# Attention's small products in halves, splits and reloads behind the last fold, and one pool of five PSUM banks

## The chip, the cores and the metric

The kernel runs on one core of one Trainium2 chip. The metric is device time in microseconds; lower is better. TensorE (PE) multiplies into PSUM, which has eight banks of 128 x 512 floats; VectorE (DVE) and ScalarE (ACT) read PSUM and write SBUF; GpSimd (POOL) works on SBUF alone; SyncE (SP) and the queues of ACT and POOL issue transfers.

## The reference

For 4 batches of 768 tokens and 8 heads of 64, each chunk of 32 tokens attends to 8 memory keys, 16 tokens to its left, itself and 8 to its right. The result, 512 channels wide, goes through a mixer along the tokens (rank 32) and a two-layer perceptron with 2048 hidden units:

```python
for c in range(nc):
    l_start, r_end = max(0, c_start - 16), min(S, c_end + 8)
    k_full = np.concatenate([mem_k, k[:, :, l_start:r_end]], axis=2)
    v_full = np.concatenate([mem_v, v[:, :, l_start:r_end]], axis=2)
    scores = scale * np.matmul(q_c, k_full.transpose(0, 1, 3, 2))
    a = softmax(scores)
    out[:, :, c_start:c_end] = np.matmul(a, v_full)
x = out.transpose(0, 2, 1, 3).reshape(B, S, H * D)
u = x + (x.transpose(0, 2, 1) @ U @ V).transpose(0, 2, 1)
return u + np.maximum(u @ w_ch1, 0.0) @ w_ch2
```

The weights arrive as 64-bit floats and are decoded on the chip.

## The kernel before

**Precision.** Each factor of the perceptron is split into a high and a low part (`split_hidden`, the pairs `th`/`tl`, `w1`/`w1l`), and three products are added in PSUM.

**Batches.** Batch 0's attention runs first and alone. Then `both_blocks` does batch 0's perceptron in 32 units, one for each token block (2) and hidden chunk (16): `w1_step` (12 matmuls, L1124), then `w2_step` of an earlier unit (nine matmuls: six L1178, three L1183). Batches 1 to 3 go through `fast(b)`: a scheme of seven products for the first projection. `products(p)` is a group of seven products of six matmuls each (L1412) for the hidden chunks 2p and 2p+1, into three banks; p runs from 0 to 7. `first_block(p)` adds their second projection for the first token block, `second_block` that for the other block, eight hidden chunks at a time, in three accumulators that live for the whole pass.

**The next batch's attention is a generator**, run a step at a time between these pieces, at *borders*. In `both_blocks` a border stands before and after `w1_step` of the units behind the 18th, and `PLAN` says how many steps each gets. In `fast` there are 40 borders: after the third and the seventh product of each group, and after each `w2_step`; `PLACES` lists those that get a step. For T = 0, 1, 2 (256 tokens each) the steps are: transposes of keys and queries (`k_part`, `q_part`, L583), scores and softmax (`s_part`), transposes of the weights (`weights_in`, L742), and weighted values (`weigh`, `av_part`). In `fast(1)` and `fast(2)`: `weigh(0)` at border 16, `s_part(1)` at 18, `q_part(2)` at 20, `weights_in(1)` at 22, `s_part(2)` at 23 (behind the last `w2_step` of `second_block`'s first pass), `weigh(1)` at 24 (behind the third product of p = 4), `weights_in(2)` at 25, `weigh(2)` at 27.

**Small products.** `s_turn` and `av_turn` each run 64 matmuls of 64 x 32 by 64 x 64 into two banks in turn (L657, L760); a trace holds two records for each, 128 in a set. There are 24 sets, 18 of them for batches 1 to 3. Behind the scores VectorE takes a maximum (L675) and a difference (L676) over each whole bank, ScalarE the exponential, VectorE the sums.

**The end of batch 0.** `prepare` makes the sums of weight chunks for the seven products, `build_factor` splits one of them (L1380 on ACT, L1381 on DVE). `recall(0, 1)` reloads the three tiles of x that the last second projection adds to (SP, L1114). `following()` drains the attention of batch 1 and then folds its tokens (`fold_both`, transposes L1333, parts L1343, `th` L1347, `tl` L1348), one third in each of the last three units; `fast(1)`'s products read `th` and `tl`.

**Order.** PE, POOL and SP run in the order of the program. DVE is ordered by hand until unit 18 and ACT until unit 2; from there a planner orders both by when inputs should be ready and by priority (`tc.high_priority`).

**PSUM.** Three banks (`ps_o`) hold accumulators. Two (`ps_h`) serve `w1_step`, two of the three banks of `products` and two of `second_block`'s accumulators; three (`ps_a`) serve attention's `att_ps`, the third bank of `products` and the other accumulators:

```python
ps_a = ctx.enter_context(tc.tile_pool(name="ps_a", bufs=3, space=PSUM))
ps_h = ctx.enter_context(tc.tile_pool(name="ps_h", bufs=2, space=PSUM))
ps_o = ctx.enter_context(tc.tile_pool(name="ps_o", bufs=1, space=PSUM))
```

Of the kernel before, what the change touches and what calls it, by code (L numbers as in the profile page):

```python
# [55 lines left out]
def chunk_attn_then_mixer_kernel(  # L56
# [46 lines left out]
    late = left.enter_context(tc.tile_pool(name="late", bufs=1))  # L103
    early = right.enter_context(tc.tile_pool(name="early", bufs=1, side="right"))
    dram = ctx.enter_context(tc.tile_pool(name="dram", bufs=1, space=bass.MemoryType.DRAM))
    ps_a = ctx.enter_context(tc.tile_pool(name="ps_a", bufs=3, space=PSUM))
    ps_h = ctx.enter_context(tc.tile_pool(name="ps_h", bufs=2, space=PSUM))
    ps_o = ctx.enter_context(tc.tile_pool(name="ps_o", bufs=1, space=PSUM))

    def slot(shape, dtype, name):  # L110
# [14 lines left out]
    def bank():  # L125
        kind = next(kinds, "a")
        if kind == "a":
            return ps_a.tile([P, 512], F32, name="ps_a")
        if kind == "h":
            return ps_h.tile([P, 512], F32, name="ps_h")  # L130
        return ps_o.tile([P, 512], F32, name="acc" + kind[1])

    warm, small = [0], [0]
# [292 lines left out]
    def attention(b, xs):  # L426
# [109 lines left out]
        def v_home(T):  # L536
            return vbs[T if b == 0 else T % 2]
# [107 lines left out]
        pT = {}  # L645

        def s_turn(T):

            qt = [qts.pop((T, h)) for h in range(2)]
            banks = [att_ps() for _ in range(2)]  # L650
            psv = [ps.rearrange("n (t k g w) -> n t k g w", t=2, k=2, g=2) for ps in banks]
            for t in range(2):
                for p in range(NPR):
                    for i in range(NI):
                        for s in range(2):
                            rows = slice(D * s, D * s + D)
                            nc.tensor.matmul(  # L657
                                out=psv[s][CK * i:CK * i + CK, t, p % 2, p // 2, :],
                                lhsT=qt[p // 2][rows, p % 2, NI * t + i, :],
                                rhs=kall[rows, NB * (T % 2) + NI * t + i, p, :], start=True, stop=True,  # L660
                            )
            return banks, psv

        def s_weights(T, banks, psv, which=range(2)):
            for s in which:
# [64 lines left out]
            nc.vector.reciprocal(out=rs, in_=rs)  # L730

        def s_part(T):
            s_weights(T, *s_turn(T))
            s_sums(T)
            s_recip(T)

        def t_part(T, s):
            pt = pts[T, s]
# [6 lines left out]
            nc.scalar.copy(out=pT[T, s], in_=psv)  # L745

        def av_part(T):
            x_part(T, av_turn(T))

        def av_turn(T):  # L750

            vt, pt = v_home(T), [pT.pop((T, s)) for s in range(2)]
            banks = [att_ps() for _ in range(2)]
            psv = [ps.rearrange("n (t j d) -> n t j d", t=2, j=4) for ps in banks]
            for t in range(2):
                for j in range(4):
                    for i in range(NI):
                        for g in range(2):
                            rows = slice(NW * g, NW * g + NW)
                            nc.tensor.matmul(  # L760
                                out=psv[g][CK * i:CK * i + CK, t, j],
                                lhsT=pt[j % 2][rows, 2 * t + j // 2, CK * i:CK * i + CK],
                                rhs=vt[rows, NI * t + i, D * j:D * j + D], start=True, stop=True,
                            )
            return psv

        def x_part(T, psv):
            rs = rss.pop(T)
# [171 lines left out]
        else:  # L940
# [13 lines left out]
            def weigh(T):  # L954
                need("v", T)
                av_part(T)
                issued.add(f"av{T}")

            def weights_in(T):
                for s in two:  # L960
# [22 lines left out]
                (weigh, (1,)), (weights_in, (2,)),  # L983
            )
            for what, args in order:
                what(*args)
                yield
            weigh(2)
            yield

        if b > 0:
            gp.append(att_ps())
# [53 lines left out]
    w1ls = {}  # L1046

    def turn_x(c):
        bank_ = ps_h.tile([P, 512], F32, name="ps_h") if c in (1, 2) else ps_o.tile([P, 512], F32, name=f"acc{int(c == 0)}")
        for tt in range(TB):  # L1050
            nc.tensor.matmul(
                out=bank_[:, tt * P:(tt + 1) * P], lhsT=xs[(0, tt)][:, c * P:(c + 1) * P],
                rhs=ident, start=(tt == 0), stop=False, is_transpose=True, skip_group_check=True,
            )
        return bank_
# [59 lines left out]

    def w1_step(b, blk, f, w1l):
        uh, ul = uT[(b, blk)]
        ph = att_ps() if f == 0 and (b, blk) == (0, 0) else ps_h.tile([P, 512], F32, name="ps_h")
# [30 lines left out]
    def w2_step(b, blk, f, where, begins, ends, hh, hl):  # L1149

        if begins:
            for tt in range(TB):
                if where == 1 or where == 2 and tt == 2:
                    accs[where, tt] = ps_a.tile([P, CH], F32, name="ps_a")
                elif where == 2:
                    accs[where, tt] = ps_h.tile([P, CH], F32, name="ps_h")
# [35 lines left out]
    def both_blocks(following):  # L1192
# [11 lines left out]
        for n, (blk, f, where, begins, ends) in enumerate(units):  # L1204
# [28 lines left out]
                open_turned()  # L1233
            if n == len(units) - 1:
                open_fast()
                for m in (3, 4):
                    build_factor(0, m)
            if n == 0:
                decode(2, 4)
                for c, g3 in rest[2:]:  # L1240
# [9 lines left out]
                border()  # L1250
            if n == len(units) - 3:
                prepare(0, True)
            if n == len(units) - 2:
                recall(0, 1)
            if n >= len(units) - 3:
                following()
            prev.append((blk, f, where, begins, ends) + hid_)
            if solo or n % 2 == 0 or ends:
                while len(prev) > (not ends):
# [5 lines left out]
    def place(n):  # L1265
        for _ in range(n):
            next(gen[0], None)
# [5 lines left out]

    at = [0]

    def border():
        place(PLAN[at[0]])
        at[0] += 1

# [86 lines left out]
    def fast_border():  # L1366
        let_go()
        serve(4)
        place(PLACES.count(passed[0]))
        passed[0] += 1  # L1370

# [21 lines left out]
    def seven(b, kept, last):  # L1393
# [3 lines left out]
        made = {}  # L1397

        def products(p):
            banks = [ps_h.tile([P, 512], F32, name="ps_h"), ps_a.tile([P, 512], F32, name="ps_a")]  # L1400
            banks.append(ps_h.tile([P, 512], F32, name="ps_h"))
# [148 lines left out]
```

## Time and profile before

| what | value |
|---|---|
| median of 3 runs | 652.95 us (651.62 to 653.56) |
| the profiled execution's own time | 654.24 us |
| its span, first to last instruction | 652.5 us |
| mean granted TensorE clock | 0.992 of 2.4 GHz |
| busy: PE, DVE, ACT, POOL | 625.3, 422.9, 305.5, 75.4 us |

The profile is of one execution. Busy time is a share of the span; a matmul's end is modelled, and matmuls overlap, so starts are compared rather than sums of durations. "L1412" is line 1412 of the kernel before. A wait is the idle time of an engine before an instruction, put down to what released it; "issue" means that nothing in the profile released it. Times in rows are microseconds from the span's start.

### The profile page before, as it was taken

To read this page: it belongs to the slowest core of one execution; us is meant where nothing else is said; L and a number is where in the kernel's file an instruction comes from. 1 tells how busy PE (TensorE), PEld (TensorE's weight loads), DVE (VectorE), ACT (ScalarE), POOL (GpSimd) and SP (SyncE) were. 2 spreads that over 40 slices of the span, in tenths; PEclk is the share of its full clock that TensorE was granted. 3 is DMA by queue.
4 is the path that set the end of the run, shared out by engine and by line. 5 is a ranking of instruction groups with operands and counts; after the bars stand their busy time and mean duration, and the time that the engine had idled before them with its cause. 6 is when DMAs were issued, how large, how long until landed. Compare 5 with 4: busy or idle time off the path is not lost.

```text
span 652.5 us, 15750 instructions
## 1 busy us (share of the span) xinstructions
PE 625.3 (96%) x6196; PEld 547.6 (84%) x6198; DVE 422.9 (65%) x889; ACT 305.5 (47%) x770; POOL 75.4 (12%) x128
## 2 busy tenths in 40 slices
PE   7788999999899899999999999999999999999997
PEld 6656999988778799878898899888988899889986
DVE  5977997887428957458676863655756875427442
ACT  4656676585215555524334554533433643315321
POOL 4700011100200722033300000000000000000000
PEclk9999999999989999999999999999999999999999
DMA  8896685695606589233361589144432663100011
GB/s 215 188 334 242 207 272 177 193 271 150 180 18 207 162 218 225 86 89 128 128 212 70 149 209 247 43 99 130 156 93 78 206 220 91 49 23 26 2 73 73
DMA packets 134357, 96.83 MB, mean 148 GB/s; under 512 B 88842, under 2 KB 111114, under 8 KB 134282
## 3 DMA queue, kind: packets, MB, share of 16 engines
q1 hardware_dynamic: 121690, 70.25, 38.9%
q10 hardware_dynamic: 9936, 17.04, 7.0%
q0 software_dynamic: 2656, 8.52, 3.9%
q8 instruction: 49, 0.80, 0.5%
q14 instruction: 26, 0.21, 0.1%
HBM read 69.44 MB, written 25.43 MB: 145 GB/s over the span
## 4 chain that ended last, share of the span: by engine, by line
PE 79%; DVE 7%; DMA 5%; issue 3%; ACT 3%; SPq 1%; POOL 0%; ACTq 0%; DVEq 0%; POOLq 0%
PE ps_h L1412 18%; PE acc L1178 13%; PE ps_a L1412 7%; PE ps_h L1124 6%; PE acc L1183 6%; PE ps_h L1178 6%; PE ps_a L1178 4%; PE ps_h L1183 3%; PE ps_a L760 2%; PE ps_a L583 2%; PE ps_a L657 2%; PE ps_a L1183 2%; PE ps_a L742 1%; DMA vb<-in_v_dram 1%; PE ps_h L1170 1%
## 5 line engine op out<-in xcount | busy, mean ns | idle before, releaser
L1178 PE MATMUL acc<-w,hh 128*128 128x512 f32 x366 | 98.5, 404 | 1.0 <-DVE w L368 1.0
L1412 PE MATMUL ps_h<-th,w1l 128*128 128x384 f32 x288 | 83.3, 342 | 2.6 <-DVE part L1429 2.6
L1178 PEld LDWEIGHTS acc<-w,hh 128*128 128x128 f32 x366 | 67.6, 190 | 15.7 <-issue 1.7
L1388 DVE SCALAR_TENSOR_TENSOR hl<-kept,hh 128x384 fp32r<-128x384 f32 x48 | 26.8, 558 | 48.9 <-PE ps_a L1183 22.4
L1412 PEld LDWEIGHTS ps_h<-th,w1l 128*128 128x128 f32 x288 | 52.8, 188 | 6.8 <-DVE part L1429 4.1
L1387 ACT ACTIVATE hh<-kept 128x384 fp32r<-128x384 f32 x48 | 25.4, 530 | 62.8 <-PE ps_a L1178 39.2
L1412 PE MATMUL ps_h<-th,s 128*128 128x384 f32 x192 | 53.0, 337 | 0.0
L1183 PE MATMUL acc<-w,hl 128*128 128x512 f32 x183 | 52.3, 394 | 0.0
L1412 PE MATMUL ps_h<-tl,w1l 128*128 128x384 f32 x144 | 48.6, 338 | 1.8 <-DVE tl L1348 1.8
L1178 PE MATMUL ps_h<-w,hh 128*128 128x512 f32 x156 | 43.0, 397 | 0.0
L1124 PE MATMUL ps_h<-uh,w1h 128*128 128x384 f32 x124 | 42.2, 346 | 0.5 <-ACT uh L1096 0.5
L1183 PEld LDWEIGHTS acc<-w,hl 128*128 128x128 f32 x183 | 34.8, 190 | 7.6
L1124 PE MATMUL ps_h<-ul,w1h 128*128 128x384 f32 x124 | 40.9, 337 | 0.0
L1178 PE MATMUL ps_a<-w,hh 128*128 128x512 f32 x132 | 37.9, 390 | 1.7 <-ACT hh L1130 1.7
L1418 ACT COPY part<-ps_h 128x384 f32<-128x384 f32 x24 | 11.5, 480 | 54.2 <-PE ps_h L1412 38.8
L1380 ACT CAST s<-sums 128x256 fp32r<-128x256 f32 x72 | 28.2, 409 | 16.6 <-PE ps_h L1412 16.6
L1412 PEld LDWEIGHTS ps_h<-th,s 128*128 128x128 f32 x192 | 35.1, 188 | 0.2 <-DVE part L1422 0.2
L1300 POOL TENSOR_TENSOR sums<-val 128x256 f32<-128x256 f32 x40 | 31.8, 818 | 28.3 <-PE ps_a L583 10.7
L1420 DVE TENSOR_TENSOR part<-ps_a,part 128x384 f32<-128x384 f32 x24 | 13.3, 554 | 31.3 <-PE ps_a L1412 29.5
L1178 PEld LDWEIGHTS ps_h<-w,hh 128*128 128x128 f32 x156 | 28.4, 188 | 5.6
L1381 DVE TENSOR_TENSOR s<-sums,s 128x256 fp32r<-128x256 f32 x72 | 32.6, 464 | 0.0
L1412 PE MATMUL ps_h<-tl,s 128*128 128x384 f32 x96 | 32.3, 336 | 0.0
(279 smaller groups left out, 1400.8 us busy)
## 6 DMA issues: line engine op xcount, KB each, us to landing
sums<-sumsd SPq DMA_DIRECT2D x32, 256.0 KB
xd<-x ACTq DMA_DIRECT2D x30, 256.0 KB
x<-xd SPq DMA_DIRECT2D x30, 256.0 KB
rw<-in_moe_w_ch_dram SPq DMA_DIRECT2D x14, 512.0 KB
vb<-in_v_dram SPq DMA_DIRECT2D x56, 98.0 KB
raw<-in_moe_w_ch_dram SPq DMA_DIRECT2D x20, 256.0 KB
qn<-in_q_dram SPq DMA_DIRECT2D x36, 128.0 KB
rw<-in_moe_w_ch_dram SPq DMA_DIRECT2D x16, 256.0 KB
```

Of the source, the lines that this page charges most:

```text
L583: nc.tensor.transpose(out=psv[:, p, r, :], in_=half[:, r, 2 * p:2 * p + 2, :].rearrange("n h d -> n (h d)"), identity=ident,)
L657: nc.tensor.matmul(out=psv[s][CK * i:CK * i + CK, t, p % 2, p // 2, :], lhsT=qt[p // 2][rows, p % 2, NI * t + i, :], rhs=kall[rows, NB * ( ...
L1124: nc.tensor.matmul(out=ph[:, :TOK], lhsT=w[:, c, :], rhs=u[c], start=(m == 0), stop=(m + 1 == len(parts)),)
L1178: nc.tensor.matmul(out=acc[tt], lhsT=h[:, sl], rhs=w, start=(begins and m == 0), stop=False,)
L1183: nc.tensor.matmul(out=acc[tt], lhsT=hl[:, sl], rhs=w2h[f], start=False, stop=ends is not None)
L1300: nc.gpsimd.tensor_tensor(out=two[:, m % 2], in0=a, in1=b_, op=getattr(ALU, op))
L1380: nc.scalar.copy(out=s[:, 0:2], in_=total)
L1381: nc.vector.tensor_tensor(out=s[:, 2:4], in0=total, in1=s[:, 0:2].bitcast(F32), op=ALU.subtract)
L1387: nc.scalar.activation(out=hh, in_=src, func=AF.Relu)
L1388: nc.vector.scalar_tensor_tensor(out=hl, in0=src, scalar=0.0, in1=hh.bitcast(F32), op0=ALU.max, op1=ALU.subtract,)
L1412: nc.tensor.matmul(out=banks[at_], lhsT=w[:, wc, :], rhs=t[:, i, c, :], start=(n < 3 and m == 0), stop=(m + 1 == len(parts)), skip_group_c ...
L1420: nc.vector.tensor_tensor(out=ta, in0=b2, in1=ta, op=ALU.subtract)
```

## The change

It does three things.

1. For batches 1 to 3, `s_part` and `av_part` run only the first half of their small products (`half(0)`, 32 matmuls); the second half and all that follows it (softmax, or the scaling of x) go on a list, `tails`, that is run at the next border, before that border's own step. Batch 0 runs both halves in one go, as before.
2. In the last unit of `both_blocks`, the reloads `recall(0, 1)` (one unit earlier before) and the splits `build_factor(0, 3)` and `(0, 4)` stand behind `following()`.
3. The pools `ps_a` and `ps_h` become one pool of five banks, `ps_b`. All places that took a tile of either take one of `ps_b` with the tag "bank" (`bank`, `turn_x`, `w1_step`, `w2_step`, `products`); only the first of them is shown.

```diff
-    ps_a = ctx.enter_context(tc.tile_pool(name="ps_a", bufs=3, space=PSUM))
-    ps_h = ctx.enter_context(tc.tile_pool(name="ps_h", bufs=2, space=PSUM))
+    ps_b = ctx.enter_context(tc.tile_pool(name="ps_b", bufs=5, space=PSUM))
...
         if kind == "a":
-            return ps_a.tile([P, 512], F32, name="ps_a")
+            return ps_b.tile([P, 512], F32, name="ps_a", tag="bank")
...
         def s_turn(T):
-
+            *turned_, rest_ = s_half(T)
+            rest_(1)
+            return turned_
+
+        def s_half(T):
             qt = [qts.pop((T, h)) for h in range(2)]
             banks = [att_ps() for _ in range(2)]
...
-            for t in range(2):
+
+            def half(t):
                 for p in range(NPR):
...
-            return banks, psv
+
+            half(0)
+            return banks, psv, half
...
         def s_part(T):
-            s_weights(T, *s_turn(T))
-            s_sums(T)
-            s_recip(T)
+            banks, psv, half = s_half(T)
+
+            def others():
+                half(1)
+                s_weights(T, banks, psv)
+                s_sums(T)
+                s_recip(T)
+
+            tails.append(others)
...
         def av_part(T):
-            x_part(T, av_turn(T))
+            psv, half = av_half(T)
+
+            def others():
+                half(1)
+                x_part(T, psv)
+                issued.add(f"av{T}")
+
+            tails.append(others)
...
             for what, args in order:
+                run_tails()
                 what(*args)
                 yield
+            run_tails()
             weigh(2)
             yield
+            run_tails()
...
             if n == len(units) - 1:
                 open_fast()
-                for m in (3, 4):
-                    build_factor(0, m)
...
-            if n == len(units) - 2:
-                recall(0, 1)
             if n >= len(units) - 3:
                 following()
+            if n == len(units) - 1:
+                recall(0, 1)
+                for m in (3, 4):
+                    build_factor(0, m)
...
+    tails = []
+
+    def run_tails():
+
+        while tails:
+            tails.pop(0)()
+
     def border():
+        run_tails()
         place(PLAN[at[0]])
...
     def fast_border():
         let_go()
         serve(4)
+        run_tails()
         place(PLACES.count(passed[0]))
```

## Rows read from the trace of the kernel before

**Rows 1.** The page: busy times, instruction queue, parts (busy us, mean ns).

```profile
PE 625.3 (96%) x6196; PEld 547.6 (84%) x6198; DVE 422.9 (65%) x889; ACT 305.5 (47%) x770; POOL 75.4 (12%) x128
...
q8 instruction: 49, 0.80, 0.5%
...
L1420 DVE TENSOR_TENSOR part<-ps_a,part 128x384 f32<-128x384 f32 x24 | 13.3, 554 | 31.3 <-PE ps_a L1412 29.5
```

**Rows 2.** TensorE's waits from 135 to 600 us (total us, times, longest us).

```profile
PE ps_a L760 <- issue: 3.1, 1, 3.1
PE ps_h L1412 <- DVE part L1429: 2.6, 5, 1.2
PE ps_h L1412 <- DVE tl L1348: 1.8, 2, 1.4
PE ps_a L583 <- ACT kall L613: 1.3, 1, 1.3
PE ps_a L657 <- issue: 0.9, 1, 0.9
...
PE ps_a L1412 <- DVE tl L1348: 0.2, 1, 0.2
```

**Rows 3.** TensorE's timeline, two stalls (start us, us, engine, line).

```profile
173.37 0.34 PE L1124 MATMUL ps_h<-uh,w1h 128*128 128x384 f32 x1
...
174.87 1.40 PE L760 MATMUL ps_a<-vb,pT 64*32 64x64 f32 x118
179.40 0.45 PE L760 MATMUL ps_a<-vb,pT 64*32 64x64 f32 x10 [3.14 <-issue]
...
281.75 1.45 PE L657 MATMUL ps_a<-kall,qt 64*32 64x64 f32 x125
284.14 0.30 PE L657 MATMUL ps_a<-kall,qt 64*32 64x64 f32 x3 [0.94 <-issue]
```

**Rows 4.** Busy times from 178.4 to 185.2 us; granted clock third from the end.

```profile
178.40:185.20 6.80, 5.80 (x26) 4.66 (x27) 1.42 (x4) 0.32 (x1) 1.91 (x3) 0.50 0.02 4
```

**Rows 5.** Transfer queues from 176.3 to 179.3 us: packets, MB, share.

```profile
q8 instruction: 1, 0.02, 2.4%
```

**Rows 6.** TensorE's timeline around one set, and without one.

```profile
152.00 0.86 PE L1183 MATMUL acc<-w,hl 128*128 128x512 f32 x3
152.79 1.48 PE L657 MATMUL ps_a<-kall,qt 64*32 64x64 f32 x128
154.20 0.44 PE L1124 MATMUL ps_h<-uh,w1h 128*128 128x384 f32 x1
154.48 0.33 PE L1124 MATMUL ps_h<-ul,w1h 128*128 128x384 f32 x1
154.65 0.34 PE L1124 MATMUL ps_h<-uh,w1h 128*128 128x384 f32 x1
...
165.35 0.86 PE L1183 MATMUL acc<-w2last,hl 128*128 128x512 f32 x3
166.05 1.53 PE L1178 MATMUL acc<-w2last,hh 128*128 128x512 f32 x6
```

**Rows 7.** TensorE's timeline, fast(1), around borders 23 to 25.

```profile
296.59 1.48 PE L657 MATMUL ps_a<-kall,qt 64*32 64x64 f32 x128
...
301.34 1.48 PE L760 MATMUL ps_a<-vb,pT 64*32 64x64 f32 x128
...
309.27 0.44 PE L1412 MATMUL ps_h<-th,w1l 128*128 128x384 f32 x1 [1.20 <-DVE part L1429]
```

**Rows 8.** VectorE's timeline behind the scores of border 23.

```profile
299.54 1.28 DVE L676 TENSOR_TENSOR pt<-ps_a,mx 128x512 f32<-128x512 f32 x2
```

**Rows 9.** VectorE's timeline at the end of batch 0.

```profile
214.38 2.73 DVE L1381 TENSOR_TENSOR s<-sums,s 128x256 fp32r<-128x256 f32 x3
217.03 1.74 DVE L1343 TENSOR_TENSOR fold<-ps_a,fold 128x256 f32<-128x256 f32 x5
```

**Rows 10.** SyncE's queue, the reloads of x.

```profile
201.59 3.69 SPq L1114 DMA_DIRECT2D x<-xd  x3
```

More of the change, by code (lines that the diff above doesn't have):

```diff
@@ L127, in bank @@
         if kind == "a":
-            return ps_a.tile([P, 512], F32, name="ps_a")
+            return ps_b.tile([P, 512], F32, name="ps_a", tag="bank")
         if kind == "h":
-            return ps_h.tile([P, 512], F32, name="ps_h")
+            return ps_b.tile([P, 512], F32, name="ps_h", tag="bank")
         return ps_o.tile([P, 512], F32, name="acc" + kind[1])
@@ L747, in av_part, with av_half @@
         def av_part(T):
-            x_part(T, av_turn(T))
+            psv, half = av_half(T)
[4 more added lines that the diff above has]
+            tails.append(others)
         def av_turn(T):
+            psv, half = av_half(T)
+            half(1)
+            return psv
+        def av_half(T):
             vt, pt = v_home(T), [pT.pop((T, s)) for s in range(2)]
@@ L754, in av_turn, with half @@
             psv = [ps.rearrange("n (t j d) -> n t j d", t=2, j=4) for ps in banks]
-            for t in range(2):
+            def half(t):
                 for j in range(4):
@@ L764, in av_turn @@
                             )
-            return psv
+            half(0)
+            return psv, half
         def x_part(T, psv):
@@ L956, in weigh @@
                 av_part(T)
-                issued.add(f"av{T}")
             def weights_in(T):
@@ L1048, in turn_x @@
     def turn_x(c):
-        bank_ = ps_h.tile([P, 512], F32, name="ps_h") if c in (1, 2) else ps_o.tile([P, 512], F32, name=f"acc{int(c == 0)}")
+        bank_ = ps_b.tile([P, 512], F32, name="ps_h", tag="bank") if c in (1, 2) else ps_o.tile([P, 512], F32, name=f"acc{int(c == 0)}")
         for tt in range(TB):
@@ L1117, in w1_step @@
         uh, ul = uT[(b, blk)]
-        ph = att_ps() if f == 0 and (b, blk) == (0, 0) else ps_h.tile([P, 512], F32, name="ps_h")
+        ph = att_ps() if f == 0 and (b, blk) == (0, 0) else ps_b.tile([P, 512], F32, name="ps_h", tag="bank")
         parts = [(w1h[f], uh, c) for c in range(NCK)] + [(w1l, uh, c) for c in range(NCK)]
@@ L1153, in w2_step @@
                 if where == 1 or where == 2 and tt == 2:
-                    accs[where, tt] = ps_a.tile([P, CH], F32, name="ps_a")
+                    accs[where, tt] = ps_b.tile([P, 512], F32, name="ps_a", tag="bank")
                 elif where == 2:
-                    accs[where, tt] = ps_h.tile([P, CH], F32, name="ps_h")
+                    accs[where, tt] = ps_b.tile([P, 512], F32, name="ps_h", tag="bank")
                 else:
@@ L1399, in products @@
         def products(p):
-            banks = [ps_h.tile([P, 512], F32, name="ps_h"), ps_a.tile([P, 512], F32, name="ps_a")]
-            banks.append(ps_h.tile([P, 512], F32, name="ps_h"))
+            banks = [ps_b.tile([P, 512], F32, name="ps_h", tag="bank"), ps_b.tile([P, 512], F32, name="ps_a", tag="bank")]
+            banks.append(ps_b.tile([P, 512], F32, name="ps_h", tag="bank"))
             banks = [bank_[:, :TOK] for bank_ in banks]
```

## The prediction

> **What bounds the kernel now.** I read the page first, then TensorE's waits, then its timeline around the longest of them, and only then the other engines at the places that the change touches. The page says that TensorE is the limit: busy 625.3 of 652.5 us [rows 1]. So whatever makes TensorE stand still, or adds work to it, is paid in full, and what the others do counts only where TensorE waits for them. The waits after the first batch's attention are few [rows 2], and the whole prize of this change is in that list. The first is for "issue", that is for nothing that an engine or a transfer of data owes. The timeline shows where [rows 3]: 118 of the 128 small matmul records of weighted values (L760) run, TensorE stands for 3.14 us, and the last ten follow. Instructions arrive in packets: 49 on the instruction queue for 6196 matmuls and 6198 weight loads, 253 for each packet [rows 1]. During the stall one such packet moves [rows 5]. I read this as code that came too late: 128 records are 256 instructions with their loads, a whole packet eaten in under 1.5 us. Counting 253 instructions back from the stall (118 pairs, and eight and a half matmuls of L1124) one is at about 173.3: that packet's worth took 6.1 us until 179.40. At the second stall, 0.94 us after 125 records, the same count goes back a matmul and a half ahead of 281.75, to about 281.4: 2.7 us until 284.14 [rows 3]. So the code of a packet is there 2.7 to 6.1 us after the packet before it was begun. The long stall costs more than itself: from 178.4 to 185.2 the granted clock is 0.50, the lower level of 1.2 GHz, with TensorE busy for 5.80 us of it, so 2.9 us more [rows 4].
>
> The Trainium skill (Runtime: NRT & Kernel Launch, section Instruction fetch mechanics) has the same blocks but holds that crossing one is "mostly hidden". Taken at its word these stalls have another cause, the halves cure nothing, and the sum below ends 5.8 us higher, 661.7. The trace disagrees: the engine waited for no one else, one packet's worth after the last crossing.
>
> **The halves: what they remove.** Each of the 18 sets of small products in batches 1 to 3 becomes two of 64 records with a border's work between. A packet's worth then holds a half, at least one step of the second projection (nine matmuls, 18 instructions, 0.70 us for three of them [rows 6], so 2.1 us) and most of the other half: 0.8 + 2.1 + 0.7 = 3.6 us or more. That cures the 2.7 us case, and the 6.1 us one to a stall of at most 2.5 us, perhaps half of that, too short for the clock. At stake are 3.14 + 0.94 + 2.9 = 7.0 us; I leave 1.2 behind and take 5.8 (ends: 3, if other packets come late since all code behind the first half shifts, and 7.0).
>
> **What they add: the switch.** A set costs more than its records [rows 6]. From the first of three L1183 matmuls to the set is 0.79 us, against 0.70 to another L1178: 0.09. From the set's start to the next matmul is 1.41 us; 1.48 less one record of 0.22 is 1.26 from first to last, so 0.14 pass after the last where a step is 0.01. The next matmul takes 0.28 instead of 0.17: 0.11. Together 0.34 us for each set, however short. Halving adds 18 sets, but at border 24 of fast(1) and fast(2) (below) two halves stand side by side, so 16: 16 x 0.34 = 5.4 us. The ends are 4.6 (0.29 where transposes stand beside a half, as their own switch is there already) and 6.1 (18). The rows speak of a fixed price at each border of the small form. The Trainium skill (TensorEngine Tiling (Array Packing), section Key Properties) says that "mode switching requires drain", and that is a rule against this change, without a price. By it the 5.4 stand; without a drain the sum would be 5.4 us lower, 650.5.
>
> **What they add: a wait for banks.** A half holds its two PSUM banks until its partner has run and VectorE has read them, one border longer than now. Five banks serve both. Mostly that fits. Not at border 24 of the fast batches: at border 23 the scores of T=2 take two banks (first half), the products of p=4 take three, and at border 24, after their third product, the change runs the second half of the scores and right behind it the first half of the weighted values of T=1, which needs two. All five are taken: the products use theirs until the seventh. So TensorE must wait until VectorE has done memset, maximum and difference on both score banks, because the records of a half alternate between two banks. Before, the scores end at 298.07 and VectorE's difference at 300.82, which is 2.75 us [rows 7, 8]; the three products between the scores and L760 at 301.34 hid it. The cover is gone: 2.75 us in fast(1) and in fast(2), 5.5 together (ends: 5.0, and 7.7 when two parts of 0.55 [rows 1] stand before the softmax each time). Behind the waiting matmul stand products four to seven, and all else on TensorE. It has no full matmul for 0.8 + 2.75 + 0.8 = 4.4 us; in [rows 3, 4] the clock fell 3.5 us after the last one, and at 281.75 a pause of 2.6 us without them left it high. I count one fall for the two places, at the 2.9 us of [rows 4]; ends are none and 5.8. At border 20 the query transposes may wait for score banks in the same way, but a step of 2.1 us lies between: 0.3 for both (0 to 1.0). Slots that are held a border longer cost nothing while the loads, which waited in their queue anyhow, stay ahead.
>
> **The one pool.** Five waits for L1429 add up to 2.6 us [rows 2]: the next group's first product must have the bank that the sixth product used. At four of these places the shared pool has two other banks free; at the fifth (309.27 [rows 7]) VectorE was late because of work that now falls into the wait at border 24. I take all 2.6 (ends 0 and 2.6: the planner chooses the bank). The second key transposes waited 1.3 us for a copy by ScalarE [rows 2]; a bank of the first projection is free there, and the first half of the scores doesn't need the last key window. I take 1.3 (0 to 1.3).
>
> **Behind the last fold.** At the end of batch 0 three splits sit on VectorE from 214.38, 2.73 us long, while the last fold's transposes are done [rows 9]; its parts start at 217.03, and the products wait for tl, 1.8 and 0.2 us in all [rows 2]. Moving two of the splits behind the fold should save most of 2.0, but two of the three splits seen come from lines that are not moved, and the planner filled a gap with them. I take 1.5 (0 to 2.0). They are next needed by the fourth and fifth product, 18 and 24 matmuls after the first. The three reloads of x go with them; on SP they pass nothing but their own wait for slots. They were issued from 201.59, 3.69 us for three [rows 10], long before the adds that read them. Issued behind the fold they may land some us late, but TensorE needs those accumulators only after the first two groups of products, 84 matmuls on, and this hides it, so I cost it at nothing; without that cover it is a rival.
>
> **Sum.** Added: 5.4 + 5.5 + 2.9 + 0.3 = 14.1. Removed: 5.8 + 2.6 + 1.3 + 1.5 = 11.2. Net +2.9 us, on the profiled execution's own 654.24 (its span is 652.5): 657.1. That execution is 1.3 over the median of the runs, 652.95, so for a median I forecast 655.9.
>
> **Rivals.**
> - No fall of the clock: both waits at border 24 are there, the clock stays. 655.9 - 2.9 = 653.0. For it: the ten other waits in [rows 2], up to 1.4 us, left the clock at full; against it: 4.4 us without a full matmul.
> - Faster: no wait at border 24, because the second half's readers finish early or a product's bank is free. Place: border 24; price: 5.5 and the 2.9 with it; it decides from the point where the wait there is under 1.5 us each, and at none the time is 647.5. For it: before, TensorE never waits for the softmax. Against it: the count of five.
> - The halves don't cure the fetch: code still arrives late, at other sets. 655.9 + 5.8 = 661.7. For it: the 6.1 us of one packet, and a packed stretch around 170 to 190 where each packet's worth takes about 5 us whatever the order; against it: the 3.6 us that a packet's worth takes at least.
> - The reloads of x land late, and VectorE's adds stand before the parts that free the product banks: I price it at 2 us (three such parts and a half of 0.55, [rows 1]): 657.9. For it: the planner doesn't know when a reload lands; against it: the loads have been early everywhere.
>
> **Chances.** Forecast 0.38, no fall 0.27, faster 0.14, fetch not cured 0.12, late x 0.09. A measurement here can tell about 0.3%, 2.0 us. Faster by more: 0.14 and 0.06 from the lower side of "no fall", 0.20. Within: the other 0.21 of that case and 0.06 of the forecast's low end, 0.27. Slower: the rest, 0.53. The range from 650.0 to 662.0 leaves out the faster rival and little else; the forecast's own range is 653.5 to 660, from 0.29 or 0.34 for a set, 5.0 to 7.7 for the banks and 1 to 2.6 for the pool.
>
> **What would show it.** Right: waits for "issue" in small products under 1 us after 135 us; 36 short sets in batches 1 to 3 with 0.34 each; at the third product of p=4 in fast(1) and fast(2) a wait of TensorE for the softmax's difference of 2.5 us or more, and a low clock behind one of them; no wait for the part that L1429 makes now; tl in time. Wrong: no wait at that place, a half that costs under 0.1 us beyond its records, or issue stalls as large as before.

## The result, and the profile after

The changed kernel takes **659.15 us** (median of 19 runs, 654.77 to 662.22) against 652.72 us (650.78 to 654.75, 19 runs) for the kernel before in the same session: a ratio of 1.0093, 95% interval 1.0073 to 1.0112. It is slower by 6.4 us; the forecast was 655.9 us, 2.9 us slower, with a range from 650 to 662. The profiled execution took 656.65 us, 2.4 us more than that of before; it is the fifth fastest of the 19.

In the new file the lines have moved: the scores are L661 (were L657), the weighted values L784 (L760), the softmax's difference L682 (L676), the products L1449 (L1412), the second projection L1206 and L1211 (L1178 and L1183), the first L1152 (L1124), the parts L1457 to L1466 (L1420 to L1429), tl L1384 (L1348), the split L1418 (L1381).

The page of after, first TensorE's busy time, then the instruction queue:

```profile
PE 629.9 (96%) x6198; PEld 548.8 (84%) x6198; DVE 419.6 (64%) x889; ACT 306.9 (47%) x770; POOL 74.2 (11%) x128
...
q8 instruction: 49, 0.80, 0.5%
```

TensorE's waits of after, 135 to 600 us (total us, times, longest us), which answer to [rows 2]:

```profile
PE ps_a L784 <- DVE pt L682: 5.3, 4, 2.4
PE ps_a L661 <- issue: 2.1, 2, 1.4
PE ps_h L1449 <- DVE tl L1384: 1.2, 1, 1.2
PE ps_a L1449 <- DVE tl L1384: 0.8, 1, 0.8
```

Read this list against the one of before. The 3.1 us stall for "issue" is gone and so is the wait of the products for the part, 2.6 us. The key transposes wait no more, but 1.4 us of "issue" has come at the first scores of batch 1. The 0.7 us of "issue" beside it is what is left of the second stall of [rows 3], now inside a half of batch 2's scores (L661 at 281.98, 0.77 us). The two waits for tl stand at 2.0 us as they did. And at the head is a wait that before did not have: the weighted values for the softmax, 5.3 us. Its place, in TensorE's timeline of fast(1) in after (start us, us, engine, line, and in brackets the idle time before), which answers to [rows 7]:

```profile
296.23 0.51 PE L1449 MATMUL ps_h<-th,w1l 128*128 128x384 f32 x2
296.67 0.86 PE L661 MATMUL ps_a<-kall,qt 64*32 64x64 f32 x64
299.90 0.27 PE L784 MATMUL ps_a<-vb,pT 64*32 64x64 f32 x2 [2.37 <-DVE pt L682]
300.49 0.83 PE L784 MATMUL ps_a<-vb,pT 64*32 64x64 f32 x62 [0.33 <-DVE pt L682]
301.25 0.69 PE L1449 MATMUL ps_h<-th,w1l 128*128 128x384 f32 x1
301.74 0.52 PE L1449 MATMUL ps_h<-tl,w1l 128*128 128x384 f32 x1
...
304.62 0.52 PE L1449 MATMUL ps_a<-th,s 128*128 128x384 f32 x2
304.97 0.34 PE L1449 MATMUL ps_h<-th,s 128*128 128x384 f32 x1
```

VectorE's timeline at the same place, which answers to [rows 8]:

```profile
297.79 0.13 DVE L675 MEMSET ps_a<- 32x32 f32 x2
297.91 1.29 DVE L681 TENSOR_REDUCE mx<-ps_a 128x8 f32<-128x512 f32 x2
299.12 1.28 DVE L682 TENSOR_TENSOR pt<-ps_a,mx 128x512 f32<-128x512 f32 x2
```

The second half of the scores ends at 297.5 (296.67 and 0.86). The first two records of the weighted values start at 299.90, when the first bank has been read, and stand again for 0.33 until the second difference is done at 300.40. Then the products run at 0.32 us a step where 0.17 or 0.18 is their usual one. The busy times of that stretch in after, the granted clock third from the end, which answers to [rows 4]:

```profile
301.20:304.60 3.40, 3.40 (x23) 3.35 (x11) 1.28 (x4) 0.78 (x2) 2.79 (x4) 0.50 0.02 5
```

The clock is at its lower level for 3.4 us, of which half, 1.7 us, is lost. In fast(2) the same wait stands at 455.36:

```profile
455.36 0.27 PE L784 MATMUL ps_a<-vb,pT 64*32 64x64 f32 x2 [2.32 <-DVE pt L682]
455.96 0.83 PE L784 MATMUL ps_a<-vb,pT 64*32 64x64 f32 x62 [0.33 <-DVE pt L682]
456.72 0.45 PE L1449 MATMUL ps_h<-th,w1l 128*128 128x384 f32 x1
```

and the clock stays high there. That is what step "a wait for banks" said, place and cause, with one fall for the two places.

### The profile page after: what moved, and what is told of

Same layout as the page of the kernel before. It is cut to its first block, busy times and chain, and to the rows that moved or that the text cites. A ratio compares the mean times of both kernels' runs of the same rounds, so it can differ in the third digit from the quotient of the medians.

```text
span 654.9 us, 15747 instructions
## 1 busy us (share of the span) xinstructions
PE 629.9 (96%) x6198; PEld 548.8 (84%) x6198; DVE 419.6 (64%) x889; ACT 306.9 (47%) x770; POOL 74.2 (11%) x128
## 4 chain that ended last, share of the span: by engine, by line
PE 88%; DMA 5%; DVE 3%; SPq 1%; issue 1%; ACT 1%; DVEq 0%; ACTq 0%
PE ps_h L1449 20%; PE acc L1206 14%; PE ps_h L1152 9%; PE ps_a L1449 8%; PE acc L1211 7%; PE ps_h L1206 6%; PE ps_a L1206 5%; PE ps_h L1211 3%; PE ps_a L582 2%; PE ps_a L1211 2%; PE ps_a L784 2%; DMA rw<-in_moe_w_ch_dram 2%; PE ps_a L661 2%; DMA vb<-in_v_dram 2%; PE ps_a L754 1%; PE ps_h L1198 1%
## 5 line engine op out<-in xcount | busy, mean ns | idle before, releaser
L1206 PE MATMUL acc<-w,hh 128*128 128x512 f32 x366 | 97.5, 401 | 1.0 <-DVE w L367 1.0
L1449 PE MATMUL ps_h<-th,w1l 128*128 128x384 f32 x288 | 84.5, 345 | 0.0
L1206 PEld LDWEIGHTS acc<-w,hh 128*128 128x128 f32 x366 | 66.7, 188 | 15.4 <-issue 1.5
L1449 PEld LDWEIGHTS ps_h<-th,w1l 128*128 128x128 f32 x288 | 53.4, 190 | 3.2 <-issue 1.7
L1449 PE MATMUL ps_h<-th,s 128*128 128x384 f32 x192 | 52.9, 336 | 0.0
L1211 PE MATMUL acc<-w,hl 128*128 128x512 f32 x183 | 51.7, 390 | 0.0
L1449 PE MATMUL ps_h<-tl,w1l 128*128 128x384 f32 x144 | 48.9, 340 | 1.2 <-DVE tl L1384 1.2
L1206 PE MATMUL ps_h<-w,hh 128*128 128x512 f32 x156 | 43.5, 401 | 0.0
L1152 PE MATMUL ps_h<-uh,w1h 128*128 128x384 f32 x124 | 42.2, 346 | 0.8 <-ACT uh L1124 0.8
L1152 PE MATMUL ps_h<-ul,w1h 128*128 128x384 f32 x124 | 40.8, 337 | 0.0
L1211 PEld LDWEIGHTS acc<-w,hl 128*128 128x128 f32 x183 | 34.4, 188 | 7.5
L1206 PE MATMUL ps_a<-w,hh 128*128 128x512 f32 x132 | 37.9, 390 | 1.8 <-ACT hh L1158 1.8
L1457 DVE TENSOR_TENSOR part<-ps_a,part 128x384 f32<-128x384 f32 x24 | 13.3, 556 | 35.8 <-PE ps_a L1449 34.6
L1449 PEld LDWEIGHTS ps_h<-th,s 128*128 128x128 f32 x192 | 35.1, 188 | 0.0
L1206 PEld LDWEIGHTS ps_h<-w,hh 128*128 128x128 f32 x156 | 28.1, 188 | 5.7
L1418 DVE TENSOR_TENSOR w1l<-sums,w1l 128x256 fp32r<-128x256 f32 x48 | 21.2, 442 | 18.0 <-ACT w1l L1417 17.8
L1449 PE MATMUL ps_h<-tl,s 128*128 128x384 f32 x96 | 32.3, 336 | 0.0
```

The source lines that it names most:

```text
L1152: nc.tensor.matmul(out=ph[:, :TOK], lhsT=w[:, c, :], rhs=u[c], start=(m == 0), stop=(m + 1 == len(parts)),)
L1206: nc.tensor.matmul(out=acc[tt], lhsT=h[:, sl], rhs=w, start=(begins and m == 0), stop=False,)
L1211: nc.tensor.matmul(out=acc[tt], lhsT=hl[:, sl], rhs=w2h[f], start=False, stop=ends is not None)
L1418: nc.vector.tensor_tensor(out=s[:, 2:4], in0=total, in1=s[:, 0:2].bitcast(F32), op=ALU.subtract)
L1449: nc.tensor.matmul(out=banks[at_], lhsT=w[:, wc, :], rhs=t[:, i, c, :], start=(n < 3 and m == 0), stop=(m + 1 == len(parts)), skip_group_c ...
L1457: nc.vector.tensor_tensor(out=ta, in0=b2, in1=ta, op=ALU.subtract)
```

## The experiments

All were timed in five rounds beside the kernel before, on the same chip within a group; edits are against the kernel after unless something else is said. Groups were timed in different sessions, so kernels of two groups are best compared by their ratios to before. "After" has 19 runs, "halves in batch 1", "batch 1 and fold" and "queries on VectorE" have 6 each, the others 12. The table gives medians, the kernel before of the same group, the ratio with its 95% interval, and the mean time that TensorE spent at the lower level of its clock (1.2 of 2.4 GHz), worked out for each run as 2 x (1 - granted clock) x span and averaged. At most half of that time is lost. It counts every fall of the clock in the kernel, also those in batch 0's attention, which no edit is aimed at.

| kernel | us | before | ratio | low clock, us |
|---|---|---|---|---|
| after | 659.15 | 652.72 | 1.0093 (1.0073 to 1.0112) | 12.0 |
| steps apart | 655.28 | 653.72 | 1.0026 (0.9993 to 1.0059) | 8.6 |
| whole sets | 650.12 | 653.72 | 0.9951 (0.9925 to 0.9977) | 9.2 |
| halves in batch 1 | 647.52 | 653.72 | 0.9906 (0.9871 to 0.9940) | 3.9 |
| fold first | 648.76 | 653.72 | 0.9922 (0.9893 to 0.9952) | 8.9 |
| no meeting | 649.89 | 654.11 | 0.9943 (0.9917 to 0.9969) | 4.9 |
| pool alone | 650.86 | 654.11 | 0.9953 (0.9928 to 0.9978) | 12.4 |
| batch 1 and fold | 646.20 | 654.11 | 0.9876 (0.9835 to 0.9917) | 3.4 |
| 128 more instructions | 651.85 | 654.11 | 0.9973 (0.9944 to 1.0001) | 9.1 |
| fold part alone | 654.32 | 652.50 | 1.0015 (0.9990 to 1.0041) | 10.1 |
| queries on VectorE | 644.10 | 652.50 | 0.9869 (0.9839 to 0.9899) | 5.1 |

**Steps apart.** The weighted values of T=1 and what follows start a border later, so that they do not meet the scores' second half at border 24.

```diff
-PLACES = [3, 5, 7, 9, 11, 13, 14, 16, 18, 20, 22, 23, 24, 25, 27, 29, 31, 32, 33, 35]
+PLACES = [3, 5, 7, 9, 11, 13, 14, 16, 18, 20, 22, 23, 25, 26, 28, 30, 31, 32, 33, 35]
```

> The changed kernel with the steps behind border 23 moved by one border (PLACES: 25, 26, 28, 30 for 24, 25, 27, 29), so that the weighted values of T=1 no longer start right behind the second half of the scores. Bank theory: the waits for L682 at border 24 (2.37 + 0.33 and 2.32 + 0.33 us in the profile) go, and the clock falls behind them: 5.4 us plus one or two falls of 1.7 us, so 0.989 to 0.992 of the changed kernel, 651.5 to 653.5 us. Rival (the switch price and late code are the whole loss): 658 us or more, as the number of sets stays 36.

The wait for the softmax is gone, but TensorE's waits show its like in another place:

```profile
PE ps_a L754 <- DVE x L798: 3.7, 2, 1.9
```

At border 26 the weighted values' second half runs, and the transposes of the next weights (L754), right behind it, want a bank that VectorE has not yet read:

```profile
305.40 0.86 PE L784 MATMUL ps_a<-vb,pT 64*32 64x64 f32 x64
308.20 1.85 PE L754 MATMUL ps_a<-ident,pt 128*128 128x128 f32 x8 [1.95 <-DVE x L798]
```

So the edit moved the meeting rather than removing it: 3.7 us of waits in place of 5.3, with 3.4 us at the lower clock behind the first of the two (308.3 to 311.7). At 655.28 us the kernel is above the 651.5 to 653.5 that were expected.

**No meeting.** Behind border 22 no attention step that asks for a bank follows a second half at the same border now.

```diff
-PLACES = [..., 22, 23, 24, 25, 27, 29, 31, 32, 33, 35]
+PLACES = [..., 22, 23, 25, 27, 28, 30, 31, 32, 33, 35]
```

> All halves kept, but the five attention steps behind border 22 stand at borders 23, 25, 27, 28 and 30, so that no step asks for banks that a half still holds. If the halves of batches 2 and 3 cost only their switches (12 more than with halves in batch 1 alone, 0.34 us each, 4.1 us) and the rest of their loss was the waits for banks with the clock falls behind them: no wait of TensorE for the softmax's difference or for the weighted values' multiplication, about 647.5 + 4.1 = 651.6 us. If halves in the stages of batches 2 and 3 lose the clock by themselves: no such waits, but still 655 us or more.

All that TensorE waits for from 135 to 600 us, with every set of the three batches still in halves:

```profile
PE ps_a L661 <- issue: 1.4, 1, 1.4
PE ps_h L1449 <- DVE tl L1384: 1.3, 1, 1.3
PE ps_a L1449 <- DVE tl L1384: 0.8, 1, 0.8
```

With it the kernel is 9.3 us faster than after, by nothing but four border numbers (by the ratios to before, 1.0093 and 0.9943, it is 9.8 us). That is 5.4 us of waits at border 24 in the profile (2.37 + 0.33 and 2.32 + 0.33), and a mean of 7.1 us less at the lower clock, half of which, 3.5 us, is lost time: 8.9 together. The two profiled executions differ by 9.6 us: 5.4 for the waits, 1.7 for the fall behind one of them, 0.8 for the stall at 281.98, and 1.7 for one fall more in batch 0's attention, ahead of all that this edit moves. The expected 651.6 was 1.7 too high.

**Whole sets.** The halves alone are undone, in all three batches; the pool and the fold part stay. Shown is `s_part`; `av_part` has the same edit.

```diff
-            tails.append(others)
+            others()
```

> The changed kernel with both halves run in one go at the first border (no tails); the one pool and the moved splits and reloads stay. Theory of the prediction: the switches (5.4), the border-24 waits (5.4) and their clock falls go, the stalls for late code come back (up to 7.0), the waits for the product bank (2.6) and the keys (1.3) stay away: 649 to 652 us. Rival (the pool or the moved splits cost the time): 656 or more.

The time is the same as in "no meeting", 650.12 against 649.89. Whole sets spare the switches but meet late code. TensorE's timeline of whole sets:

```profile
175.78 0.39 PE L784 MATMUL ps_a<-vb,pT 64*32 64x64 f32 x16
178.76 0.32 PE L784 MATMUL ps_a<-vb,pT 64*32 64x64 f32 x8 [2.59 <-issue]
```

and 0.67 us more at 281.76. Corrected for the time at the lower clock "no meeting" is 1.7 us the longer (649.9 - 2.5 = 647.4 against 650.3 - 4.6 = 645.7, from the means). Against that, the profile of whole sets has 4.6 us of waits that the one of "no meeting" hasn't: 3.3 of issue stalls, 0.9 more for tl and 0.4 for the part. So 18 more sets cost about 6.3 us, 0.35 each, an estimate from one profile of each kernel; the forecast had 0.34. The timeline of "no meeting" shows the price directly:

```profile
150.88 0.86 PE L1211 MATMUL acc<-w,hl 128*128 128x512 f32 x3
151.66 0.86 PE L661 MATMUL ps_a<-kall,qt 64*32 64x64 f32 x64
152.45 0.45 PE L1152 MATMUL ps_h<-uh,w1h 128*128 128x384 f32 x1
152.73 0.33 PE L1152 MATMUL ps_h<-ul,w1h 128*128 128x384 f32 x1
```

From its start to the next matmul a half takes 0.79 us, so two take 1.58 where a whole set takes 1.41 [rows 6]: 0.17 more. The 0.08 ahead of a half (0.78 against 0.70) and the 0.11 behind it (0.28 against 0.17) come a second time too: 0.36 for each added set.

**Halves in batch 1.** Batches 2 and 3 run whole sets; again `av_part` has the same edit as `s_part`.

```diff
-            tails.append(others)
+            tails.append(others) if b == 1 else others()
```

> The changed kernel with halves only in batch 1's attention (inside both_blocks, where the 3.14 us stall was); batches 2 and 3 run whole sets. Six added sets instead of 18, no wait at border 24. Theory: against the whole sets +2.0 us for six switches, less what the halves save of the 3.14 us stall and its clock fall: 648 to 652 us, below the whole sets if that stall is in most executions. Rival (halves cure nothing): 2 us over the whole sets.

It is faster than whole sets by 2.6 us and than "no meeting" by 2.4, with intervals that overlap. Beyond the clock the gain is nothing: less 2.0 for 3.9 us it is 645.7, as whole sets. The six switches, some 2 us, would eat the 2.6 us stall at 178.76, which is gone; what is left is 5.3 us less at the lower clock. Whether that comes from the stall is not shown: in the profile of whole sets the clock fell near 31 and 219 us, and stayed high behind this stall.

**128 more instructions.** Whole sets, and ahead of batch 1's first scores 32 matmuls whose result is overwritten.

```diff
+            if (b, T) == (1, 0):
+                for _ in range(32):
+                    nc.tensor.matmul(
+                        out=banks[0][0:32, 0:64], lhsT=ident[0:64, 0:32], rhs=ident[0:64, 0:64],
+                        start=True, stop=True,
+                    )
```

> Whole sets, with 32 matmuls (32 columns by 64, into a bank that the next products overwrite) ahead of batch 1's first scores: 128 more TensorE instructions and about 0.7 us of work, with no other edit. If the stalls for issue come from code that arrives 256 instructions at a time: the 2.6 us stall near 178.8 us and the 0.7 us one near 281.8 are gone, and stalls stand at the end of the weighted values near 161 us and of the scores near 295 us, where 256 instructions are eaten in 1.5 us; their place in the count of instructions leaves the same remainder by 256 as before. If they come from something else at those moments (transfers, other engines): they stay near 179 and 282 us. Time: 650.1 + 0.7, give or take 3 us.

If code comes in blocks, the stalls must stand at one remainder of the instruction count and move in the kernel when something is put ahead. They do. (Lines stand 7 lower in the file here: L791 are the weighted values, L1159 the first projection.) At 178.87 and 278.50 whole sets run without a gap; the first is:

```profile
178.87 1.48 PE L791 MATMUL ps_a<-vb,pT 64*32 64x64 f32 x128
```

and there are new ones, one behind the weighted values near 164 us and one inside those near 450 us:

```profile
162.79 1.28 PE L791 MATMUL ps_a<-vb,pT 64*32 64x64 f32 x99
164.00 0.45 PE L1159 MATMUL ps_h<-uh,w1h 128*128 128x384 f32 x1
165.06 0.44 PE L1159 MATMUL ps_h<-ul,w1h 128*128 128x384 f32 x1 [0.61 <-issue]
```

```profile
447.14 1.38 PE L791 MATMUL ps_a<-vb,pT 64*32 64x64 f32 x116
450.63 0.33 PE L791 MATMUL ps_a<-vb,pT 64*32 64x64 f32 x12 [2.11 <-issue]
```

The number in TensorE's stream (matmuls, weight loads and its queue's own entries) of the first instruction after each stall:

```
before              4543 = 17 x 256 + 191    6591 = 25 x 256 + 191
after                                        6593 = 25 x 256 + 193
whole sets          4545 = 17 x 256 + 193    6593 = 25 x 256 + 193
128 more            4033 = 15 x 256 + 193   10433 = 40 x 256 + 193
```

The two of before are 8 x 256 apart, the new two 25 x 256, and all keep the remainder of their kernel: the packet's worth that the prediction took as 253 is 256. The expected stall near 295 us did not come, so not each block that is eaten in 1.5 us is late. The same remainders stand in batch 0, whose sets no edit here cuts: TensorE stops for 1.48 us at number 1471 = 5 x 256 + 191 in before (29.93 us) and for 1.74 us at 705 = 2 x 256 + 193 in after (18.19 us). The extra matmuls took 3.7 us and not 0.7, but 1.4 of it falls into the wait of batch 1's first scores, which does not show here; so about 2.3 us of the time is theirs.

**Pool alone.** The kernel before with `ps_a` and `ps_h` as one pool of five banks, everywhere that the change has it, and nothing else.

```diff
-    ps_a = ctx.enter_context(tc.tile_pool(name="ps_a", bufs=3, space=PSUM))
-    ps_h = ctx.enter_context(tc.tile_pool(name="ps_h", bufs=2, space=PSUM))
+    ps_b = ctx.enter_context(tc.tile_pool(name="ps_b", bufs=5, space=PSUM))
```

> The kernel before with the five banks as one pool and nothing else. If the pool is all that the whole-set version gained (the fold part nothing): no wait for the products' last part, TensorE's waits for it (2.6 us) gone, and the time of the whole-set version, about 3.6 us under before, 650.1 us. If moving the splits and reloads gave its 1.5 us after all: about 651.6 us. If the planner takes the same banks as before: 653.

It is 3.3 us faster than before and within the uncertainty of whole sets. The waits for the part are gone, and so is the one of the key transposes; those for tl grew from 2.0 to 3.1 us. But the scores of batch 1 wait 1.4 us for "issue" here too, so that is the pool's doing and not the halves'. It also spent 3.8 us more at the lower clock than before did in its group (12.4 against 8.6), so beyond the clock the gain is nearer to 5.

**Fold part alone.** The kernel before with `recall` and the last two splits behind `following`, and nothing else.

```diff
-                for m in (3, 4):
-                    build_factor(0, m)
...
-            if n == len(units) - 2:
-                recall(0, 1)
             if n >= len(units) - 3:
                 following()
+            if n == len(units) - 1:
+                recall(0, 1)
+                for m in (3, 4):
+                    build_factor(0, m)
```

> The kernel before with the two late splits and the reloads of x put behind the last fold, and nothing else. If the order of the lines does not decide where the splits run (the planner puts them ahead of the fold again): three splits in one block ahead of the last fold on VectorE, TensorE still waiting about 2 us for tl, the time of before within 0.3%, about 653.5 us. If the forecast's 1.5 us is hidden by something in the other edits: waits for tl under 0.7 us and 652 us or less.

No gain. VectorE's timeline at the end of batch 0 shows why, beside [rows 9]:

```profile
213.93 2.73 DVE L1381 TENSOR_TENSOR s<-sums,s 128x256 fp32r<-128x256 f32 x3
216.58 1.73 DVE L1343 TENSOR_TENSOR fold<-ps_a,fold 128x256 f32<-128x256 f32 x5
```

The same three splits stand in one block ahead of the last fold, whatever the order of the lines; in after they stand there as well (210.03, then the fold at 212.68). By the program the tiles named `s` are those of the fifth, sixth and seventh product, so only one of the three, the fifth's, comes from a moved line.

**Fold first.** Whole sets, and each of the late splits gets a true dependence on the last fold: a copy of one element of its low part into the place that the split then fills.

```diff
...
+        if p == 0 and n > 2 and not guarded.get(n):
+            guarded[n] = True
+            nc.vector.tensor_copy(out=s[0:1, 0, 0:1], in_=turned[0][1][0:1, 4, 1, TOK - 1:TOK])
         nc.scalar.copy(out=s[:, 0:2], in_=total)
```

> The whole-sets kernel with the splits of chunk pair 0 for the fourth to seventh product made to wait for the last tl of the fold (one element of tl is copied into each split's tile first; it is overwritten). Theory: the move in the change failed because the planner still put three splits ahead of the last fold (210.03, 2.73 us); with the order forced the waits for tl (1.2 + 0.8 us) go: 1.5 to 2.0 us under the whole sets. Rival (the fold is late for another reason, or the splits are late in turn): no difference, or slower by 1 us with TensorE waiting for a split.

Of 3.0 us of waits for tl in the profile of whole sets none is left, and the late splits cost 0.9 in their place:

```profile
PE ps_h L1452 <- ACT s L1420: 0.9, 1, 0.9
```

The median is 1.4 us under that of whole sets. The intervals of the two overlap, but the same step on top of "halves in batch 1" gave 1.3 us again, in another session. The profiled executions don't show the gain (649.84 against 648.60): in this one the late code at the weighted values took 3.7 us.

**Batch 1 and fold.** The edit of "halves in batch 1" and that of "fold first" in one kernel:

```diff
-            tails.append(others)
+            tails.append(others) if b == 1 else others()
...
+            nc.vector.tensor_copy(out=s[0:1, 0, 0:1], in_=turned[0][1][0:1, 4, 1, TOK - 1:TOK])
```

> Halves in batch 1 alone, and the three late splits of batch 0 made to wait for the last fold. If the wait for tl and the halves of batch 1 are independent: both waits for tl (1.6 and 0.8 us) gone, perhaps 0.9 for the splits in their place, about 647.5 - 1.4 = 646.1 us. If the splits only move the wait: 647.5 us.

It takes 646.20 us after 647.52 without the second edit, as the first of the two theories had it (646.1), and no wait for tl is left in its profile.

**Queries on VectorE.** "Batch 1 and fold", with both copies of batch 1's first query transposes on VectorE.

```diff
-                q_part(T, h, (nc.scalar.copy, nc.vector.tensor_copy)[h])
+                q_part(T, h, nc.vector.tensor_copy)
```

> Halves in batch 1 alone and the splits behind the fold, as in the best version so far, and both copies of batch 1's first query transposes on VectorE, where one was on ScalarE. If the 1.4 us that TensorE stands in front of batch 1's first scores is a wait for ScalarE, which does four operations of the decoding between the last key copy and the query copies: the wait is under 0.5 us and the time 646.2 - 1.0 to 1.4, about 645 us. If that stall is late code: 1.4 us again at the same place, 646.2 us. If VectorE is late in its turn: some wait stays, 646 us.

In after, ScalarE's timeline ahead of the stall reads as follows, with decoding between the last key copy and the query copies; the last line is TensorE's:

```profile
139.05 0.41 ACT L612 COPY kall<-ps_a 128x168 f32<-128x168 f32 x1
139.24 0.52 ACT L230 ACTIVATE vb<-rw 128x256 int32<-128x256 uint32 x1
139.56 0.50 ACT L230 ACTIVATE vb<-raw 128x256 int32<-128x256 uint32 x1
139.88 0.50 ACT L216 ACTIVATE dec<-rw 128x256 f32<-128x256 f32 x1
140.20 0.50 ACT L216 ACTIVATE dec<-raw 128x256 f32<-128x256 f32 x1
140.52 0.74 ACT L642 COPY qt<-ps_a 128x256 f32<-128x256 f32 x2
...
141.07 0.96 PE L661 MATMUL ps_a<-kall,qt 64*32 64x64 f32 x64 [1.37 <-issue]
```

With the copies on VectorE the scores follow at once, in TensorE's timeline:

```profile
138.67 0.86 PE L1211 MATMUL acc<-w,hl 128*128 128x512 f32 x3
139.46 0.86 PE L661 MATMUL ps_a<-kall,qt 64*32 64x64 f32 x64
```

So that "issue" was no late code but a wait for ScalarE that the view could not name: when the key transposes no longer stood for their bank, the scores came to stand for the query copies behind the same queue. The 0.9 us of "issue" that this profile still has stand in batch 2's scores (276.08 us), where the late code of [rows 3] stood. The median of 644.10 is the best here, 1.3% under before; against 646.20 of another session its ratio to before is the same within the intervals, so the 1.4 us are shown in the timeline and not in the time.

## Why the prediction was right, and where its sum was off

The forecast, slower through a wait for banks at border 24 with a clock fall behind it, holds, and three of the four rivals don't: the wait is there (so not "faster"), the 3.14 us stall is cured, and no wait for x shows in after. "No fall" is half right in the profiled execution, where one of the two places kept its clock, and by the mean time at the lower clock wrong over the runs. Term by term, in us, added ones positive:

| step | forecast | measured | by |
|---|---|---|---|
| wait at border 24, two batches | +5.5 | +5.4 | timeline of after; "no meeting" has none |
| clock fall there | +2.9 | +3.5 | 12.0 against 4.9 us at the lower clock, halved |
| border 20 | +0.3 | 0 | no such wait in after |
| switches less late code | 5.4 - 5.8 = -0.4 | -0.2 | "no meeting", which has 18 sets more, against whole sets |
| pool and key transposes | -2.6 - 1.3 = -3.9 | -3.3 | pool alone against before |
| behind the last fold | -1.5 | 0 | fold part alone: +0.15%, interval -0.10 to +0.41 |
| sum | +2.9 | +5.4 | after against before: +6.4 |

The 1.0 between 5.4 and 6.4 is within the intervals of these rows. Of the 2.5 between the two sums the last fold has 1.5, the clock and the pool 0.6 each.

**Waits for banks and the count of five.** Right. Two score banks and three product banks are five, and the second half's readers need memset, maximum and two differences: 297.5 to 299.90 and then 300.40, 2.7 us in all where 2.75 was read off [rows 8]. Two edits of the steps' places show the count to be the cause: moved to another meeting the wait reappears for another reader, moved to none it is gone.

**The clock.** One fall for two places in the profile, as forecast, but it is half as long as the one that gave the price: 3.4 us at the lower level against 6.8 in [rows 4], so 1.7 us lost and not 2.9. Over the runs the difference is 7.1 us, as much as two such falls, 3.5 lost. That 2.9 came near 3.5 is luck: one fall was too few, and its price too high. How much of the 7.1 belongs to border 24 is not shown run by run, because falls in batch 0's attention are counted in it; the same stretch of after and of "no meeting", with 6.8 and 3.4 us at the lower level:

```profile
17.00:36.00 19.00, 15.50 (x483) 11.88 (x482) 16.68 (x42) 11.71 (x31) 11.56 (x21) 0.82 0.76 171
17.00:36.00 19.00, 15.57 (x582) 11.78 (x585) 16.35 (x45) 12.66 (x34) 11.25 (x21) 0.91 0.83 200
```

**Late code and switches.** The step was right that this is code in packets: stalls sit at a fixed remainder by 256 of the instruction count and move with 128 instructions. That a half with a step behind it outlasts a packet held for the long stall; the short one, which the prediction took as cured, kept 0.77 us in after. The Trainium skill (Runtime: NRT & Kernel Launch, section Instruction fetch mechanics) gives blocks of 256 instructions, which this agrees with, and calls the crossing "mostly hidden", which does not hold at 2.59 and 2.11 us in a set of small products. Set against the switches the cure comes to nothing: "no meeting" equals whole sets. The Trainium skill (TensorEngine Tiling (Array Packing), section Key Properties) says that "mode switching requires drain", without a price; the runs agree that each border of the small form has a price, and put it at about 0.35 us a set, with 64 records as with 128.

**Behind the last fold: the step that failed.** "I take 1.5 (0 to 2.0)" should have been the lower end. The doubt stood beside it (two of three splits come from lines that are not moved), and the run of this part alone shows that the planner put all three ahead of the fold wherever the lines stood: the waits for tl stayed at 1.7 us there and at 2.0 in after. The size was near: made to wait by a true dependence, the splits gave 1.4 and 1.3 us in the medians, though neither is clear of its interval.

**The keys: a gain that moved.** The key transposes' 1.3 us went, as forecast, and came back as 1.4 us at the scores. The step looked at what those scores need of the keys and not at the copies of the queries, which stand behind keys and decoding on ScalarE.

## What to carry to other kernels

Splitting a unit of work lengthens the life of what it holds; count the buffers at the border where the second half meets the next unit's first, and if they are all taken, the readers' whole time falls onto the path. Before a removed wait is counted as a gain, follow the engine that ended it to the next thing that it owes: if that is in the same queue, the wait moves. Check in the trace that a line moved in the source has moved on the engine; a planner may put it where it was. Here a true dependence held it.

## What the runs showed of the hardware that was not expected

- A pause of TensorE does not decide on its clock alone: in one execution of after the same 2.3 us wait with a half set on each side was followed by 3.4 us at the lower level in fast(1) and by none in fast(2). The 2.59 us stall ahead of the last eight weighted values of one set left the clock at full in whole sets and was followed by 3.4 us at the lower level in "pool alone"; behind the 3.14 us one of before it was 6.8 [rows 4]. The busy times of that stretch, whole sets first:

```profile
178.40:185.20 6.80, 6.44 (x127) 5.66 (x135) 1.66 (x5) 1.56 (x3) 1.87 (x3) 1.00 0.01 3
178.40:185.20 6.80, 5.99 (x33) 5.08 (x34) 1.42 (x4) 1.07 (x2) 2.21 (x4) 0.75 0.01 4
```

- Records of one shape can differ five times in price. The 32 extra matmuls, all on the same rows of the array and into the same place of one bank, took 3.70 us for 63 records, 59 ns each, with the granted clock at 1.00, where a set's 128 records of that shape take 1.48 us, 12 ns each. The set changes rows and bank with every matmul and columns with every second one; which of them makes it quick was not tried. TensorE's timeline of "128 more instructions":

```profile
140.52 3.70 PE L658 MATMUL ps_a<-ident 64*32 64x64 f32 x63
```
